# LSH attention, MoE and a dense SoLU layer on one core: all dense layers behind the last MoE

## Chip, core and metric

The kernel runs on one core of one Trainium2 chip. The metric is the device time of one execution in microseconds (us). The engines of the core are TensorE (PE, with its weight loads listed apart as PEld), VectorE (DVE), ScalarE (ACT), GpSimd (POOL) and SyncE (SP), which issues the DMAs. In the profile all of the kernel's instructions carry one line, L391 (the helper that emits them; L396 in the changed kernel), so groups of instructions are told apart by the names of their tiles.

## The reference

Three layers follow one another. Attention takes 2 x 8 heads of 768 rows with head width 64; a pair of row and column counts only where both fall in the same bucket of six sign bits. Its output, 1536 rows of 512, goes through four experts, and then through the dense layer.

```python
mask = q_bucket[:, :, :, None] == k_bucket[:, :, None, :]     # sign bits of q @ proj, k @ proj
scores = np.where(mask, scale * (q @ k.T), -1e9)
x = softmax(scores) @ v                                       # -> [1536, 512]

p = domain_probs / (domain_probs.sum(-1, keepdims=True) + 1e-09)
for e in range(4):                                            # w1 512 x 1024, w2 1024 x 512
    y += p[:, e:e + 1] * (np.maximum(x @ w1[e], 0) @ w2[e])

h = y @ w_in                                                  # 512 x 1024
solu = h * softmax(h)
ln = (solu - mean(solu)) / np.sqrt(var(solu) + 1e-06) * g_ln
out = ln @ w_out                                              # 1024 x 512
```

w_in, w_out and g_ln come as 64-bit floats, which the kernel decodes with integer operations into 32-bit ones; all else is float32.

## The kernel before

**Chunks.** The 1536 rows are worked on in four chunks of three tiles of 128 rows (`CHUNKS`, line 20), called 0 to 3 here. For each chunk there are three stages: attention (`attn_steps`, 1082), MoE (`moe_a`, 1277, the first product and the relu; `moe_b`, 1328, the second product and the sum over experts), and the dense layer. The main loop (1597 to 1660) runs MoE(c), then dense(c), and so on. The attention of a later chunk is laid between their steps by `Fill` (1561): attention(1) runs beside MoE(0), attention(2) beside dense(0) and MoE(1), attention(3) beside dense(1) and MoE(2). Attention(0) comes first, with nothing beside it but the loads.

**Pairs.** A product of float32 matrices is made of three matmuls of float16 halves: high times high, high times low, low times high. A matrix is split by a scaled copy to float16 (ACT, POOL or DVE) and a subtraction of the copy from the original (DVE). Scales come from row or matrix maxima (`amax`, 603; `fit_to`, 606, turns a column of maxima on PE into one factor). In chunk 0 the MoE runs with unsplit scales: its weights are kept as 32-bit pairs, and the largest of each expert is taken in passing (`wm`), so that the later chunks can use float16.

**Attention.** A row tile of one head is a row of 768 scores in PSUM. DVE takes the maximum (`sm<-PS`), ACT the exponential into `p`, then come a scaled copy `hl` in float16, a fused DVE instruction for the low half (`hl<-p,sm,hl`, scaling and subtraction in one), and a DMA that turns both halves into `t`. There are two `hl` buffers (`hl16_r`, 486) and three of `t`. When three rows stand turned, 12 short products with the values give the head's output, `xp`. So 24 rows make a chunk.

**Weights.** Two streams (`Stream`, 1181) load raw weights in pieces of 512 KB (`wra`, `wrb`), two buffers each, and split each into halves (`wsa`, `wsb`; as float16 `wsa0h`, `wsa1h` and so on, four slots each, `ws16_r`, 518). Every chunk loads and splits the MoE's 32 pieces, and the dense layer's eight: four of `winD`, four of `woutD`.

**Dense layer of chunks 0 to 2.** `y_fit` (1352) scales the rows of y by their maxima; `y_transposes` (1363) turns them on PE (`idn,y`, four 128x128 turns a tile) and splits them out of PSUM. `h2_piece` (1389) makes the first product; `ln_tiles` (1408) makes the exponential (`ee`), the softmax and the LayerNorm (`ln`) for the three tiles at once. For chunks 0 and 1 `ln_a` (1473) turns ln on PE (`idn,ln`), `ln_b` (1485) makes the second product; for chunk 2 `ln_turn` (1449) turns ln by DMA instead. While `ln_tiles` runs, the first steps of MoE(c+1) and of attention give PE work. Chunk 3 has a function of its own, `last_layer` (1501), which works tile by tile.

**Decoding.** `decode_a` and `decode_b` (1167, 1177) decode w_in and w_out beside MoE(0) and dense(0), and write them to memory as `winD` and `woutD`, from where each chunk loads them.

**Order.** The operations are recorded in program order and sent out by `emit` (376) in an order that a table of numbers sets (`ORDER`). Further tables choose the engine where an operation has several forms ("AVG": ACT, DVE or POOL) and the PSUM bank. Each engine works through its own instructions in that order; a waiting instruction holds up all that follow on its engine.

Of the kernel before, what the change touches and what calls it, by code (L numbers as in the profile page):

```python
# [8 lines left out]
F32 = mybir.dt.float32  # L9
# [386 lines left out]
def lsh_attention_moe_solu(  # L396
# [30 lines left out]
    TURN = 2  # L427
# [1267 lines left out]
```

## Time and profile before

| | before |
|---|---|
| median of 3 runs | 902.07 us (900.07 to 903.45) |
| profiled execution, whole | 897.96 us |
| its span | 895.8 us |
| PE busy | 852.7 us (95%) |
| DVE busy | 752.4 us (84%) |
| ACT busy | 488.2 us (54%) |
| mean granted clock of TensorE | 0.983 |

The profile is one execution. A busy time counts the time in which an engine had an instruction running; matmuls overlap, so their mean durations add up to more than the time between their starts. "Idle before" is the time in which an engine stood still ahead of an instruction, and the name behind "<-" is what released it. DMA share is the mean busy share of the core's 16 DMA engines. The granted clock is a share of TensorE's full speed.

In time, the stages of before are: attention(0) to about 120 us, MoE(0) with attention(1) to about 330, dense(0) from there, the others after it, and the last dense layer from about 860.

### The profile page before, as it was taken

The numbers are of one execution on the slowest core, as the hardware profiler recorded it, in microseconds if no ns is written. First come the engines' busy times: TensorE is split into PE (matmuls) and PEld (weight loads), VectorE is DVE, ScalarE is ACT, GpSimd is POOL, SyncE is SP. The second block draws the span as 40 slices with busy tenths as digits, with TensorE's granted clock in tenths as the row PEclk, the third lists the DMA queues.
The fourth block names the chain that finished last, engine by engine and source line by source line (L and its number), as shares of the span: only waits on it lengthen the run. The fifth ranks groups of instructions, "written<-read, shape, count | busy, mean of one in ns | idle before, by whom it ended". The sixth has DMA issues, their size and how long they took to land.

```text
span 895.8 us, 13401 instructions
## 1 busy us (share of the span) xinstructions
PE 852.7 (95%) x4549; PEld 547.0 (61%) x4549; DVE 752.4 (84%) x1377; ACT 488.2 (54%) x894; POOL 250.6 (28%) x302
## 2 busy tenths in 40 slices
PE   6889899998899996999999999999999999999998
PEld 5778699876688553555566555555565555455543
DVE  6888898998999999878899889887887687556595
ACT  4798346567775676644485558544463365212232
POOL 2556443554545111333224202102230010101110
PEclk9699999999999997999999999999999999999999
DMA  7877778999999887769999979587968347733400
GB/s 179 243 187 193 268 236 198 265 259 260 233 276 327 280 270 243 191 178 265 248 227 250 277 199 239 150 227 222 236 150 188 116 141 175 220 134 118 165 24 36
DMA packets 224916, 185.67 MB, mean 207 GB/s; under 512 B 137424, under 2 KB 190032, under 8 KB 224848
## 3 DMA queue, kind: packets, MB, share of 16 engines
q1 hardware_dynamic: 224848, 184.82, 75.7%
q8 instruction: 36, 0.59, 0.3%
q14 instruction: 32, 0.26, 0.1%
HBM read 128.68 MB, written 19.73 MB: 166 GB/s over the span
## 4 chain that ended last, share of the span: by engine, by line
PE 72%; DVE 12%; ACT 5%; issue 4%; DMA 3%; POOL 2%; SPq 2%; POOLq 0%; DVEq 0%; ACTq 0%
PE PS L391 72%; DVE ln L391 2%; DVE sm L391 2%; SPq L391 2%; ACT p L391 1%; DVE st L391 1%; POOL sm L391 1%; DMA t<-in_v_dram 1%; DVE hl L391 1%; DMA wrb<-in_moe_w_dram 1%; DMA t320h<-hl 1%; DMA t<-hl 1%; DVE wm L391 1%; DVE y L391 1%; ACT ee L391 1%
## 5 line engine op out<-in xcount | busy, mean ns | idle before, releaser
L391 ACT ACTIVATE p<-PS,sm 128x768 f32<-128x768 f32 x96 | 95.0, 990 | 32.8 <-DVE sm L391 22.5
L391 DVE TENSOR_REDUCE sm<-PS 128x1 f32<-128x768 f32 x96 | 91.0, 950 | 18.2 <-PE PS L391 17.5
L391 POOL TENSOR_SCALAR sm<-sm 128x1 f32<-128x1 f32 x113 | 51.7, 457 | 179.5 <-DVE sm L391 139.9
L391 PEld LDWEIGHTS <-wsa1h 128*128 128x128 f16 x576 | 55.7, 98 | 40.4 <-issue 1.2
L391 PEld LDWEIGHTS <-wsa0h 128*128 128x128 f16 x576 | 55.5, 98 | 39.4 <-issue 1.3
L391 DVE SCALAR_TENSOR_TENSOR hl<-p,sm,hl 128x768 f16<-128x768 f32 x72 | 72.7, 1011 | 5.8 <-ACT hl L391 3.8
L391 ACT ACTIVATE hha0h<-PS 128x384 f16<-128x384 f32 (+1 forms) x79 | 38.1, 492 | 72.1 <-PE PS L391 72.1
L391 PEld LDWEIGHTS <-hha0h 128*128 128x128 f16 x484 | 44.7, 98 | 50.0 <-issue 4.6
L391 PE MATMUL PS<-wsb1h,hha0h 128*128 128x512 f16 x248 | 73.9, 380 | 0.0
L391 PE MATMUL PS<-kB,qB 80*128 80x384 f32 x192 | 67.2, 350 | 6.2 <-DMA qB<-qD 3.7
L391 PE MATMUL PS<-xh,wsa 128*128 128x384 f32 x256 | 70.2, 340 | 1.9 <-POOL wsa L391 0.9
L391 PE MATMUL PS<-wsb0h,hha0h 128*128 128x512 f16 x236 | 70.4, 380 | 0.9 <-ACT y L391 0.8
L391 PE MATMUL PS<-xh1h,wsa1h 128*128 128x384 f16 x256 | 67.5, 326 | 0.0
L391 PE MATMUL PS<-xh1h,wsa0h 128*128 128x384 f16 x256 | 67.2, 326 | 0.0
L391 PE MATMUL PS<-kC,qC 128*128 128x384 f32 x144 | 57.2, 397 | 6.0 <-ACT p L391 5.5
L391 DVE SCALAR_TENSOR_TENSOR hxa0h<-PS,hha0h 128x384 f16<-128x384 f32 x64 | 35.0, 551 | 24.2 <-ACT hha0h L391 23.8
L391 ACT ACTIVATE sm<-sm 128x1 f32<-128x1 f32 x96 | 23.4, 249 | 47.8 <-POOL sm L391 24.2
L391 PEld LDWEIGHTS PS<-xh,wsa 128*128 128x128 f32 x256 | 46.6, 188 | 4.4 <-POOL wsa L391 1.6
L391 DVE SCALAR_TENSOR_TENSOR wsb0h<-wrb,fit,wsb0h 128x1024 f16<-128x1024 f32 x32 | 41.8, 1306 | 7.8 <-ACT wsb0h L391 7.4
L391 DVE SCALAR_TENSOR_TENSOR wsa1h<-wra,fit,wsa1h 128x1024 f16<-128x1024 f32 x32 | 41.0, 1282 | 7.4 <-POOL wsa1h L391 4.1
L391 PE MATMUL PS<-wsb1h,hxa0h 128*128 128x512 f16 x124 | 47.0, 379 | 0.0
L391 DVE SCALAR_TENSOR_TENSOR wsb1h<-wrb,fit,wsb1h 128x1024 f16<-128x1024 f32 x32 | 40.9, 1278 | 6.9 <-POOL wsb1h L391 4.7
(301 smaller groups left out, 2241.2 us busy)
## 6 DMA issues: line engine op xcount, KB each, us to landing
wra<-in_moe_w_dram SPq DMA_DIRECT2D x64, 512.0 KB, 5.0
wrb<-in_moe_w_dram SPq DMA_DIRECT2D x64, 512.0 KB, 4.4
kC<-kD SPq DMA_DIRECT2D x24, 384.0 KB, 4.7
wra<-winD SPq DMA_DIRECT2D x16, 512.0 KB, 5.3
wrb<-woutD SPq DMA_DIRECT2D x16, 512.0 KB, 4.6
vr<-in_v_dram SPq DMA_DIRECT2D x30, 192.0 KB, 4.5
kB<-kD SPq DMA_DIRECT2D x24, 240.0 KB, 4.4
qD<-stk SPq DMA_DIRECT2D x27, 192.0 KB, 3.1
```

The costliest lines, as they stand in the source:

```text
L391: fn(**{key: self.now(x) for key, x in kw.items()})
```

## The change

All four dense layers stand behind MoE(3) in one function, `dense`. It runs over the 12 tiles one after the other: `first(i)` makes the first product, the softmax and the LayerNorm of a tile, `second(i)` its output product, two tiles later (`lag = 2`). Four pieces of `winD` and four of `woutD` are loaded and split once, and stay in the eight `ws16_r` slots. `y_fit` now writes the scaled rows of y as a pair of float16 halves, as soon as a tile's MoE is done, and two DMAs turn them; ln is copied and subtracted into halves and turned by two DMAs in each tile but the last, whose ln PE turns. `y_transposes`, `h2_piece`, `ln_turn`, `ln_a`, `ln_b` and `last_layer` are gone.

Decoding is one pass of 16 units beside MoE(3), through the `ln` buffer. The scales of the MoE and dense weights come from sums of squares (ACT or DVE) with one small matmul in `fit_norm`, in place of maxima with a turn. In attention, `p` is scaled in place, copied to float16, and subtracted, as three instructions (scaling and copy on ACT, DVE or POOL, subtraction on DVE or POOL), in place of a scaled copy and a fused subtraction. `Fill` spreads the attention of a chunk over the steps of one MoE alone, attention(2) over MoE(1) and attention(3) over MoE(2), since no dense layer stands between them. MoE(3) has no attention beside it, as before.

The instructions on PE that turn y go from 57 to 9, those that turn ln from 90 to 26. DVE's instructions go from 1297 to 1378, counted as the order below counts them.

**The order on DVE, at the last rows of attention(2).** `p` holds exponentials, `hl` a row's float16 halves, `sm` row sums and maxima, `vr` raw values, `hxa` the relu's low half, `wra`/`wrb` raw weights, `ys` the row maxima of y. Before:

```order
L391 TENSOR_SCALAR hl_81<-p_78,sm_90 128x768
L391 TENSOR_REDUCE sm_92<-PS 128x1
L391 RECIPROCAL sm_91<-sm_91 128x1
L391 SCALAR_TENSOR_TENSOR hl_81<-p_78,sm_90,hl_81 128x768
L391 SCALAR_TENSOR_TENSOR hxa0h<-PS,hha0h 128x384
L391 SCALAR_TENSOR_TENSOR wsb1h<-wrb_103,fit,wsb1h 128x1024
L391 TENSOR_SCALAR hl_80<-p_79,sm_91 128x768
L391 SCALAR_TENSOR_TENSOR hl_80<-p_79,sm_91,hl_80 128x768
L391 SCALAR_TENSOR_TENSOR wsa1h<-wra_101,fit,wsa1h 128x1024
L391 RECIPROCAL sm_92<-sm_92 128x1
L391 SCALAR_TENSOR_TENSOR xp_98<-PS,tmp_99 64x384
L391 TENSOR_TENSOR hl_65<-vr_73,hl_65 128x3x64
```

And after:

```order
L396 CAST hl_80<-p_78 128x768
L396 TENSOR_TENSOR hl_80<-p_78,hl_80 128x768
L396 RECIPROCAL sm_91<-sm_91 128x1
L396 TENSOR_TENSOR hl_65<-vr_73,hl_65 128x3x64
L396 CAST hl_81<-p_79 128x768
L396 RECIPROCAL sm_92<-sm_92 128x1
L396 TENSOR_TENSOR hl_81<-p_79,hl_81 128x768
L396 CAST hl_80<-p_77 128x768
L396 TENSOR_TENSOR hl_80<-p_77,hl_80 128x768
L396 SCALAR_TENSOR_TENSOR xp_97<-PS,tmp_99 64x384
L396 CAST hl_65<-vr_73 128x3x64
L396 TENSOR_REDUCE ys<-y_112 128x1
```

Before, splits of MoE weights and the relu's halves stand between the rows; after, the last rows stand in a row, behind the last instruction of MoE(1), and the maximum of a y tile follows them.

**The order on PE, from the first product of the dense layer to its output product.** `xh1h` and `xl1h` are the halves of the turned y, `wsa1h` of w_in, `wsb0h` of w_out; `hha0h` and `t_82` hold turned ln. Before, in the last layer, where the turns of ln follow the products of the third tile:

```order
L391 LDWEIGHTS xh1h
L391 MATMUL PS<-wsa1h,xh1h 128x512
L391 LDWEIGHTS xl1h
L391 MATMUL PS<-wsa1h,xl1h 128x512
L391 MATMUL PS<-idn,ln_113 128x128 x4
L391 LDWEIGHTS hha0h
L391 MATMUL PS<-wsb0h,hha0h 128x512
```

And after, at the first output product:

```order
L396 LDWEIGHTS xh1h
L396 MATMUL PS<-wsa1h,xh1h 128x512
L396 LDWEIGHTS xl1h
L396 MATMUL PS<-wsa1h,xl1h 128x512
L396 LDWEIGHTS t_82
L396 MATMUL PS<-wsb0h,t_82 128x512
```

The turns on PE are gone from between the two products; ahead of the rows after stand 144 matmuls of the first product, six tiles, before the output product of the first.

The diff, cut to its core (`ORDER` and the other two tables are new throughout):

```diff
--- before.py
+++ after.py
 ORDER = """
-3 14 0 12 13 12 1 43 43 21 0 37 20 1 11 22 20 16 20 4 16 10 16 29 26 15 15 1 8 1 13 22 4 19 11 10 58 10 16 5
...
+3 0 12 12 0 11 22 0 21 25 10 11 23 5 18 13 1 33 17 16 17 10 1 14 15 26 14 21 7 13 1 6 1 19 1 9 4 16 8 12 4 2 2
...
-    XA, WA = 16.0, 4.0
+    XA, WA, YA = 16.0, 160.0, 16.0
...
+    def squares(out, in_):
+
+        n = in_.shape[1]
+        d = dump_r.next()[:, 0:n]
+        forms = dict(
+            A=("activation", dict(out=d, in_=in_, func=ACTF.Square, accum_out=out)),
+            V=(
+                "scalar_tensor_tensor",
+                dict(out=d, in0=in_, scalar=1.0, in1=in_, op0=ALU.mult, op1=ALU.mult, accum_out=out),
+            ),
+        )
+        rec.add([(name, *forms[name]) for name in "AV"])
...
+    def fit_norm(x, j, limit):
+
+        n, m = x.shape[1:]
+        ps = a_b.next()[:, 0:n * m]
+        b, t = big[:, j:j + n], fit[:, j:j + n]
+        T.matmul(out=ps, lhsT=one, rhs=x, start=True, stop=True)
...
-        yT[c] = tuple(t.bitcast(F16)[:, :, 0:TM] for t in x)
+        lower, upper = (tuple(flat16(t)[:, i * KD * TM:(i + 1) * KD * TM].rearrange("p (k q) -> p k q", k=KD) for t in x) for i in range(2))
+        yT[c] = upper if c < 2 else lower
         if c:
-            xT[c] = yT[c]
+            xT[c] = lower
...
                 hl16 = hl16_r.next()
                 h16, l16 = hl16[:, 0], hl16[:, 1]
-                times_by("AGV", h16, p, st[:, 4:5])
-                V.scalar_tensor_tensor(out=l16, in0=p, scalar=st[:, 4:5], in1=h16, op0=ALU.mult, op1=ALU.subtract)
+                times_by("AGV", p, p, st[:, 4:5])
+                copy_by("AGV", h16, p)
+                sub_by("VG", l16, p, h16)
                 o = rr * 128
                 SP.dma_start_transpose(
                     out=d16.rearrange("p a r q -> p (a r) q")[:, :, o:o + 128],
...
-            amax(dm[:, cols[i]:cols[i] + 1], w)
+            squares(dm[:, cols[i]:cols[i] + 1], w)
...
-        return decode_steps(units + out_units(0, OUT0, n), n, ln_r.next().rearrange("p a n -> p (a n)"), range(12))
-
-    def decode_b():
-        return decode_steps(out_units(OUT0, NF2, 256), 256, y_r.next().rearrange("p a n -> p (a n)"), range(12, 20))
+        return decode_steps(units + out_units(0, NF2, n), n, ln_r.t[0].rearrange("p a n -> p (a n)"), range(16))
...
-                    amax(wm[:, 2 * e + self.kind - 1, i:i + 1], t, AX.XY)
+                    squares(wm[:, 2 * e + self.kind - 1, i:i + 1], t.rearrange("p a n -> p (a n)"))
...
+        add_moe1(c, 0, NP)
+        add_moe2(c, 0, NP)
+    for j in range(FF2 // 256):
+        i1["in", j] = len(W1.items)
+        W1.items.append(winD[j])
+    for j in range(NF2 // 2):
+        i2["out", j] = len(W2.items)
+        W2.items.append(woutD[j])
...
     def y_fit(c, t):
         y = y_t[c][:, t]
-        top, by, back = (ys[:, c % 2, i, t:t + 1] for i in range(3))
+        top, by = (ys[:, c, i, t:t + 1] for i in range(2))
         amax(top, y)
-        V.tensor_scalar(out=top, in0=top, scalar1=1e-30, scalar2=1.0 / XA, op0=ALU.max, op1=ALU.mult)
+        V.tensor_scalar(out=top, in0=top, scalar1=1e-30, scalar2=None, op0=ALU.max)
         V.reciprocal(out=by, in_=top)
-        times_by("AVG", y, y, by)
-        if c == NC - 1:
-            V.tensor_tensor(out=by, in0=by, in1=fit[:, NM:NM + 1], op=ALU.mult)
-        V.tensor_tensor(out=back, in0=top, in1=big[:, NM:NM + 1], op=ALU.mult)
-
-    def y_transposes(c, t, ps):
+        power(by, by, YA)
+        V.reciprocal(out=top, in_=by)
+        y16 = hl16_r.next()[:, :, 0:DM]
+        times_by("AVG", y16[:, 0], y, by)
+        less_by("V", y16[:, 1], y, by, y16[:, 0])
+        for a in range(2):
+            SP.dma_start_transpose(out=yT[c][a][:, :, t * 128:t * 128 + 128], in_=y16[:, a])
...
-    def y_transposes(c, t, ps):
...
-    def h2_piece(c, j):
...
-    def ln_turn(c):
...
-    def ln_a(c, s):
...
-    def ln_b(c, s):
...
-    def last_layer(c):
...
+    def dense():
+
+        o_b = Bank(PS, 1, range(8), 2)
         t_b, h2_b = Bank(PS, 1, range(8), 3), Bank(PS, 2, (6, 4, 0, 2), 3)
+        tiles = [(c, t) for c in range(NC) for t in range(chunks[c][2])]
+        ln, mx = ln_r.t[0], mx_r.t[0]
+        for j in range(FF2 // 256):
+            W1.split(i1["in", j])
         parts = {}
 
+        def first(i):
+            c, t = tiles[i]
+            if t == 0:
+                V.tensor_scalar(out=ys[:, c, 1], in0=ys[:, c, 1], scalar1=fit[:, NM:NM + 1], scalar2=None, op0=ALU.mult)
+                V.tensor_scalar(out=ys[:, c, 2], in0=ys[:, c, 0], scalar1=big[:, NM:NM + 1], scalar2=None, op0=ALU.mult)
             h = h2_b.next()
+            m = mx[:, i % NT]
             for j in range(FF2 // 256):
                 h2_mm(c, t, j, h[:, j // 2])
                 if j % 2 == 1:
+                    V.tensor_reduce(out=m[:, j // 2:j // 2 + 1], in_=h[:, j // 2], axis=AX.X, op=ALU.max)
             hv = h.rearrange("p a n -> p (a n)")
+            l = ln[:, i % NT]
+            ln_tiles(m.unsqueeze(1), [(hv, l, l, hv)], [ys[:, c, a, t:t + 1] for a in (1, 2)])
+            if i < len(tiles) - 1:
+                x = t16_r.t[i % 3].rearrange("p a r q -> p (a r q)")
+                x16, y16 = x[:, 0:2 * FF2], x[:, 2 * FF2:4 * FF2].rearrange("p (a k q) -> p a k q", a=2, q=128)
+                hi, lo = x16[:, 0:FF2], x16[:, FF2:2 * FF2]
+                copy_by("AVG", hi, l)
+                sub_by("VG", lo, l, hi)
+                for a, y in enumerate((hi, lo)):
+                    SP.dma_start_transpose(out=y16[:, a], in_=y)
+                parts[i] = [[y16[:, a, k] for a in range(2)] for k in range(NF2)]
+            else:
+                gh, gl = (cuts(x[0], 512) + cuts(x[1], 512) for x in (hh_t, hx_t))
+                parts[i] = []
+                for g in range(2):
+                    ps = t_b.next()
+                    with rec.group():
+                        for a in range(4):
+                            k = g * 4 + a
+                            T.transpose(out=ps[:, a * 128:a * 128 + 128], in_=l[:, k * 128:k * 128 + 128], identity=idn)
+                    acopy(gh[g], ps)
+                    sub(V, gl[g], ps, gh[g])
+                    parts[i] += [[y[g][:, a * 128:a * 128 + 128] for y in (gh, gl)] for a in range(4)]
+
+        def second(i):
+            c, t = tiles[i]
             o = o_b.next()
+            for k in range(NF2):
+                wh, wl = W2.get(i2["out", k // 2])
+                hh, hl = parts[i][k]
+                with rec.group():
+                    for m, (a, w) in enumerate(((hh, wh), (hh, wl), (hl, wh))):
+                        T.matmul(out=o, lhsT=a, rhs=w[:, k % 2, :], start=(k == 0 and m == 0), stop=(k == NF2 - 1 and m == 2))
             store(c, t, o)
+
+        lag = 2
+        for i in range(len(tiles) + lag):
+            if i < len(tiles):
+                first(i)
+            if i >= lag:
+                second(i - lag)
...
+        if c == NC - 1:
+            dec_it = decode()
+        for s in range(NS):
+                fill.start(c + 2, NS - 1)
+            if c == NC - 1 and s % DI == 0:
+                next(dec_it, 0)
+            if c == NC - 1 and s == 17:
+                fit_norm(dm[:, 0:8].unsqueeze(1), NM, WA)
+    for _ in dec_it:
+        pass
+    fit_norm(dm[:, 8:16].unsqueeze(1), NM + 1, WA)
+    V.tensor_scalar(out=ob, in0=big[:, NM + 1:NM + 2], scalar1=1.0 / P10, scalar2=None, op0=ALU.mult)
+    dense()
```

## Rows read from the trace of the kernel before

**Rows 1.** The page's busy times: time, share of the span, instructions.

```profile
PE 852.7 (95%) x4549; PEld 547.0 (61%) x4549; DVE 752.4 (84%) x1377; ACT 488.2 (54%) x894; POOL 250.6 (28%) x302
```

**Rows 2.** Stretches: length; PE, PEld, DVE, ACT, POOL busy us (instructions); clock; DMA share; GB/s.

```profile
0.00:120.00 120.00, 100.60 (x536) 85.62 (x537) 101.83 (x196) 74.62 (x158) 59.48 (x96) 0.91 0.80 219
...
160.00:260.00 100.00, 90.08 (x461) 73.85 (x460) 94.54 (x167) 70.66 (x137) 53.57 (x46) 1.00 1.02 254
...
340.00:360.00 20.00, 11.99 (x52) 7.31 (x50) 18.71 (x59) 12.43 (x27) 3.36 (x4) 0.74 0.75 235
360.00:540.00 180.00, 179.85 (x986) 103.34 (x987) 155.40 (x261) 100.68 (x183) 53.18 (x73) 1.00 0.90 231
540.00:700.00 160.00, 158.78 (x864) 89.82 (x863) 137.53 (x235) 83.53 (x152) 27.18 (x33) 1.00 0.80 204
700.00:860.00 160.00, 160.00 (x844) 82.70 (x843) 106.47 (x160) 56.40 (x84) 14.87 (x13) 1.00 0.46 143
860.00:896.00 36.00, 31.42 (x156) 15.31 (x154) 25.16 (x86) 12.21 (x20) 0.84 (x2) 1.00 0.06 23
```

**Rows 3.** Groups on PE: tiles, shapes, count, busy us, mean ns, idle before.

```profile
L391 PE MATMUL PS<-idn,ln 128*128 128x128 f32 x90 | 15.4, 307 | 5.4 <-DVE ln L391 4.2 <-DVE wsa L391 1.0
...
L391 PE MATMUL PS<-idn,y 128*128 128x128 f32 x57 | 8.6, 274 | 0.0
```

**Rows 4.** Timeline of PE at a turn of y: start us, length us, instruction.

```profile
302.52 0.38 PE L391 MATMUL PS<-wsa1h,xl0h 128*128 128x512 f16 x1
302.74 0.60 PE L391 MATMUL PS<-idn,y 128*128 128x128 f32 x4
303.17 0.59 PE L391 MATMUL PS<-wsa1h,xh0h 128*128 128x512 f16 x2
```

**Rows 5.** Chain of waits, 176 to 260 us: start us, length us, what ran.

```profile
177.65 5.90 DMA t320h<-hl
...
239.11 5.84 DMA t<-hl
```

**Rows 6.** Groups on DVE and ACT over the span, columns as in rows 3.

```profile
L391 DVE SCALAR_TENSOR_TENSOR wsa1h<-wra,fit,wsa1h 128x1024 f16<-128x1024 f32 x32 | 41.0, 1282 | 7.4 <-POOL wsa1h L391 4.1 <-ACT wsa1h L391 3.2
L391 DVE TENSOR_REDUCE wm<-wrb 128x1 f32<-128x1024 f32 x16 | 19.4, 1209 | 0.2 <-DMA wrb<-in_moe_w_dram 0.2
L391 DVE TENSOR_REDUCE wm<-wra 128x1 f32<-128x1024 f32 x16 | 19.3, 1208 | 2.4 <-DMA wra<-in_moe_w_dram 2.4
L391 DVE SCALAR_TENSOR_TENSOR ln<-ln 128x512 int32<-128x512 int32 (+1 forms) x24 | 17.6, 738 | 1.0 <-ACT ln L391 0.9
L391 DVE SCALAR_TENSOR_TENSOR hl<-p,sm,hl 128x768 f16<-128x768 f32 x72 | 72.7, 1011 | 5.8 <-ACT hl L391 3.8 <-POOL hl L391 1.6
L391 DVE TENSOR_SCALAR hl<-p,sm 128x768 f16<-128x768 f32 x21 | 12.9, 614 | 1.8 <-DMA t<-hl 1.6
L391 DVE TENSOR_TENSOR ln<-ln,ee 128x1024 f16<-128x1024 f32 x3 | 3.7, 1223 | 0.1
L391 ACT ACTIVATE p<-PS,sm 128x768 f32<-128x768 f32 x96 | 95.0, 990 | 32.8 <-DVE sm L391 22.5 <-POOL sm L391 7.4 <-DVE hxa0h L391 0.7
```

**Rows 7.** Maxima of score rows on DVE, in 140 to 240 and 360 to 500 us.

```profile
L391 DVE TENSOR_REDUCE sm<-PS 128x1 f32<-128x768 f32 x19 | 17.9, 948 | 2.4 <-PE PS L391 2.4
...
L391 DVE TENSOR_REDUCE sm<-PS 128x1 f32<-128x768 f32 x23 | 21.8, 951 | 7.3 <-PE PS L391 7.2
```

**Rows 8.** Turns of `hl`, all of the span: from issue to landing.

```profile
DMA to landing us min/median/max: 3.6/4.8/8.2
```

**Rows 9.** Chain of waits, 334 to 361 us, columns as in rows 5.

```profile
340.30 1.24 ACT ee L391 x2
...
351.82 0.82 DVE ln L391
```

**Rows 10.** Chain of waits, 860 us to the end.

```profile
873.76 0.60 DVE mx L391
...
884.56 7.58 PE PS L391 x38
```

More of the change, by code (lines that the diff above doesn't have):

```diff
@@ L559, in sub_by, with ops_by @@
         rec.add([(name, "tensor_tensor", dict(out=out, in0=a, in1=b, op=ALU.subtract)) for name in names])
+    def ops_by(names, out, in_, a, b, op0, op1):
+        args = dict(out=out, in0=in_, scalar1=a, scalar2=b, op0=op0)
+        if op1 is not None:
+            args.update(op1=op1)
+        rec.add([(name, "tensor_scalar", args) for name in names])
     def less_by(names, out, in_, by, b):
@@ L604, in amax @@
         V.tensor_reduce(out=out, in_=in_, axis=axis, op=ALU.max, apply_absolute_value=True)
[L606 to L621 removed]
+    dump_r = Ring(0, tiles=[flat16(t32_r.t[0])[:, 2 * R * TM + i * 1024:2 * R * TM + i * 1024 + 1024] for i in range(4)])
@@ new lines, in fit_v @@
+    def fit_v(b):
+        ts = [t.rearrange("p a r q -> p (a r q)").bitcast(F32)[:, 0:H // 2 * R * D] for t in t16_r.t[0:2]]
+        for i, t in enumerate(ts):
+            SP.dma_start(
+                out=t.rearrange("p (h x) -> p h x", h=H // 2),
+                in_=v[b, i * H // 2:(i + 1) * H // 2].rearrange("h (p r) d -> p h (r d)", r=R),
+            )
+            amax(vm[:, i:i + 1], t)
+        ps = a_b.next()
+        j = 2 * E + b
+        x, y, top = big[:, j:j + 1], fit[:, j:j + 1], vm[0:1, 2:3]
+        V.tensor_reduce(out=x, in_=vm[:, 0:2], axis=AX.X, op=ALU.max)
+        T.transpose(out=ps[0:1, 0:128], in_=x, identity=idn)
+        V.tensor_reduce(out=top, in_=ps[0:1, 0:128], axis=AX.X, op=ALU.max)
+        V.tensor_scalar(out=top, in0=top, scalar1=1e-30, scalar2=None, op0=ALU.max)
+        T.matmul(out=ps[:, 256:257], lhsT=one[0:1], rhs=top, start=True, stop=True)
+        V.reciprocal(out=y, in_=ps[:, 256:257])
+        power(y, y, XA)
+        V.reciprocal(out=x, in_=y)
+        if b:
+            for e in range(E):
+                fit_p(b, e)
@@ L636, in fit_w @@
     def fit_w(e):
[L637 removed]
+        fit_norm(wm[:, 2 * e:2 * e + 2], 2 * e, WA)
         fit_p(0, e)
[L640 to L652 removed]
     def consts_a():
@@ L1210, in split @@
                 if c:
-                    w = [x.rearrange("p (a n) -> p a n", a=t.shape[1]) for x in ws16_r[self.kind].next()]
+                    w = ws16_r[self.kind].next()
+                    w = [x.rearrange("p (a n) -> p a n", a=t.shape[1]) for x in w]
                     j = NM + self.kind - 1 if m is None else m // (NF // 2) * 2 + self.kind - 1
@@ L1385, in h2_mm, with ln_tiles @@
                     m += 1
[L1387 to L1408 removed]
+    def ln_tiles(mx, tiles, back):
         n = len(tiles)
@@ L1471, in store @@
         SP.dma_start(out=out[b * S:(b + 1) * S].rearrange("(p r) d -> p r d", r=R)[:, r0 + t], in_=ot)
-    def ln_a(c, s):
-        n = chunks[c][2]
-        if c == TURN:
-            g, i = divmod(s, NF2 // 2)
-            hT["l", c, s] = [turned[g][:, a, i, 0:128 * n] for a in range(2)]
-            return
-        ps = h_b.next()
-        with rec.group():
-            for t in range(n):
-                T.transpose(out=ps[:, t * 128:(t + 1) * 128], in_=ln_t[c][:, t, s * 128:(s + 1) * 128], identity=idn)
-        hT["l", c, s] = split_h(ps, 128 * n, False)
@@ L1485, in ln_b @@
-    def ln_b(c, s):
-        b, r0, n = chunks[c]
-        m, j = divmod(s, 2)
-        i = i2["out", c, m]
-        w = W2.get(i)
-        hh, hl = hT.pop(("l", c, s))
-        mm2(("l", c), range(n), hh, hl, w, j, s == 0, s == NF2 - 1)
-        if s == NF2 - 1:
-            for t in range(n):
-                o = acc["l", c][t]
-                store(c, t, o)
-        if j == 0:
-            W2.split(i + 1)
-        else:
-            W2.load(i + 2)
-    def last_layer(c):
-        n = chunks[c][2]
-        ln_t[c] = ln_r.next()
-        mx_t[c] = mx_r.next()
-        y_b, o_b = Bank(PS, 1, range(8), 1), Bank(PS, 1, range(8), 2)
+    def dense():
+        o_b = Bank(PS, 1, range(8), 2)
@@ L1507, in last_layer @@
         t_b, h2_b = Bank(PS, 1, range(8), 3), Bank(PS, 2, (6, 4, 0, 2), 3)
-        gh, gl = (Ring(0, tiles=cuts(x[0], 512) + cuts(x[1], 512)) for x in (hh_t, hx_t))
+        tiles = [(c, t) for c in range(NC) for t in range(chunks[c][2])]
+        ln, mx = ln_r.t[0], mx_r.t[0]
+        for j in range(FF2 // 256):
+            W1.split(i1["in", j])
         parts = {}
-        def transposes(t):
-            parts[t] = []
-            for g in range(2):
-                ps = t_b.next()
-                with rec.group():
-                    for i in range(4):
-                        s = g * 4 + i
-                        T.transpose(
-                            out=ps[:, i * 128:i * 128 + 128], in_=ln_t[c][:, t, s * 128:(s + 1) * 128], identity=idn
-                        )
-                hh, hl = gh.next()[:, 0:512], gl.next()[:, 0:512]
-                acopy(hh, ps)
-                sub(V, hl, ps, hh)
-                parts[t].append((hh, hl))
@@ L1538, in last_layer @@
-        for t in range(n):
-            if t == 0:
-                transposes(0)
-            if t + 1 < n:
-                transposes(t + 1)
-            o = o_b.next()
-            for g in range(2):
-                hh, hl = parts[t][g]
-                for i in range(4):
-                    s = g * 4 + i
-                    wh, wl = W2.get(i2["out", c, s // 2])
-                    with rec.group():
-                        for m, (a, w) in enumerate(((hh, wh), (hh, wl), (hl, wh))):
-                            T.matmul(
-                                out=o,
-                                lhsT=a[:, i * 128:i * 128 + 128],
-                                rhs=w[:, s % 2, :],
-                                start=(s == 0 and m == 0),
-                                stop=(s == NF2 - 1 and m == 2),
-                            )
-            store(c, t, o)
+            l = ln[:, i % NT]
@@ L1597, in lsh_attention_moe_solu @@
     fill.start(1, NS - 10)
-    a0 = 0
     for c in range(NC):
-        end = NS - (LB if c == NC - 1 else 0)
-        for s in range(a0, end):
+        if c == NC - 1:
+            dec_it = decode()
+        for s in range(NS):
             if s == NS - LA and c + 1 < NC:
-                fill.start(c + 2, NS + 1)
+                fill.start(c + 2, NS - 1)
             a_to(c, s + LA + 1)
```

222 lines of the change are left out of this document (45 added, 177 removed), and 205 rows, old and new, of the table ORDER.

## Prediction

> **What bounds the kernel now.** I read the page's busy shares first. TensorE (PE) is busy 852.7 of 895.8 us and VectorE (DVE) 752.4 [rows 1], so two things can shorten the kernel: less PE work, or fewer stalls of PE. The table by stretches says where the stalls are [rows 2]: PE idles 19 us in the first 120 us (the first chunk's attention, which the change leaves alone), 9.9 us in 160 to 260, 8.0 us in 340 to 360, and 4.6 us in the last 36. From 360 to 860 it is idle 1.4 us in 500, so there every microsecond saved must come out of PE's own instructions, and any new stall is paid in full.
>
> The two stalls differ. In 160 to 260 DVE is busy 94.5 of 100 us and the DMA share stands at its ceiling, 1.02; the chain of waits goes through 5.9 us landings of attention rows [rows 5]. In 340 to 360 the chain runs through the LayerNorm of chunk 0, from an exponential at 340.30 to the last scaling at 351.82 [rows 9], while the work meant to cover it has run out; the granted clock falls to 0.74 there.
>
> The sum is made against the profiled execution: span 895.8 us, 897.96 us with what lies around it. The median of the three runs, 902.07, is 4.1 above that; I add it at the end.
>
> **The change part by part.**
>
> *Turns taken from PE.* Gone are 48 transposes of y and 64 of ln (90 to 26 and 57 to 9 in the order). Four in a row take from 302.74 to 303.17, so 0.108 us each [rows 4], and 112 are 12.1 us. The busy column would give 0.15 and 0.17 each [rows 3], 18 us in all, but that counts waits and overlap. They stand in stretches where PE does not idle, so all of it counts: **-12** (-18 to -12). The matrix work of the dense layers is the same.
>
> *Weights split once.* 24 loads of 512 KB and 24 splits go, some 31 us of DVE (1.28 each [rows 6]) plus the scaling on ACT or POOL. After 360 PE is the bound, so there this gives nothing by itself.
>
> *Chunk 0's stage relieved.* Out of the first MoE go 38.7 us of maxima over weights (now mostly squares on ACT) and the decoding, whose largest DVE group is 17.6 us [rows 6]. Against that stand ten more subtractions of weight halves at some 1.2 us each. From the first to the last score row of chunk 1 the order holds 134 us of DVE work before and 107 after (counts times the mean durations of the trace; small instructions overlap, so the busy time is some 8% less), while PE has 604 matmuls before and 670 after, 121 us at the spacing of an unstalled stretch (986 in 180 us [rows 2], 0.18 each). DVE stops being the bound. The stall of 9.9 us, with some 4 us of refilling after its many stops, goes for the most part: **-11** (-14 to 0). What is late next is PE itself.
>
> *Chunk 0's LayerNorm stall.* Nothing dense stands in the middle any more, so the 8.0 us of idling and 2 to 3 us at the fallen clock go: **-11** (-12 to -8).
>
> *Attention packed tighter.* This is the new cost. Before, the rows of chunk 2 ran beside dense(0) and MoE(1), 23 of them from 360 to 500 [rows 7], 6.1 us each. After, PE's order between the first and last score of chunk 2 holds only 433 matmuls instead of 709, 78 us of work or 3.3 us a row, and the last six rows stand behind the last matmul of MoE(1) (the order section shows DVE there: casts and subtractions in a row with nothing of MoE between). DVE's work for the same 24 rows, counted the same way, is 91 us. Of that, the new subtraction in place of the fused one (1.01) is bounded by that row and by 0.75 of 1.22, the same subtraction at 1024 columns [rows 6]; I take 0.97, and 0.61 for the cast from the scaling of equal shape. One row also holds one of two hl slots for cast 0.6, subtraction 1.0 and a landing of 4.8 [rows 8], so the ring allows 3.2 us a row, 77 us. So 88 to 91 us for 78: 10 to 13 us of stall. Behind it waits the whole of MoE(2): its first 72 matmuls need all eight heads. The drain after the last score (maximum 0.95 [rows 7], exponential 0.99 [rows 6], scaling, cast and subtraction 2.5, landing 4.8, 12 products 2, evacuations and small steps 3: some 14 us, with 7 us of PE work behind it) lies in the same stretch. **+12** (0 to +40). The rows of chunk 3 have 694 matmuls, 125 us of PE, for 113 of DVE: **+3** (0 to +8) for the drain at the end of MoE(2).
>
> *Decoding moved to the last MoE.* In 700 to 860 DVE was busy 106.5 of 160 and the DMA share 0.46 [rows 2]. The order gives DVE 112 us there for 130 us of PE: hidden. If that cover failed, up to 50 us of DVE work would show.
>
> *The dense tail.* Twelve tiles of 48 matmuls at 0.22 us [rows 4], 10.4 us a tile on PE. DVE needed 25 us for the three tiles of the last layer [rows 2], 8.4 each, so PE remains the bound. A tile's chain takes some 11 us (from the second maximum at 873.76 to the first transposes at 884.56 [rows 10]); with copy, subtraction and landing it is 18 to 19 us, against 20 us of other tiles between its two halves. PE starts with six tiles of first products, before any output product (order, second place), while the output weights are split; that start may leave **+4** (0 to +12). The SP queue gets 34 more DMA turns and 24 fewer loads; in the tail it has little else. The end is as before: the last tile still turns on PE, with 14 us of output products in front.
>
> The Trainium skill speaks against this part: the page "VectorE: DVE Perf Modes", section "The three transpose paths", gives a 128x128 turn as 390 ns on TensorE and 1309 ns by DMA, and its rules prefer TensorE where PSUM will do as destination. At 1309 ns one after another, the 272 blocks now turned by DMA for y and ln would be an estimate of 356 us. The trace disagrees: 12 blocks land in 4.8 us, 0.40 each.
>
> **Sum.** 895.8 - 12 - 11 - 11 + 12 + 3 + 4 = 881 us of span, 883 with the 2.2 around it, **887** at the level of the median, 1.7% less than before. What a measurement of this kernel can tell from no change is about 0.5%, 4.5 us.
>
> **The rivals.**
>
> *Landings bound the packed rows (slower).* If the row transposes of chunk 2 land not in 4.8 but in 8.2 us, the longest seen [rows 8], a row takes (1.6 + 8.2) / 2 = 4.9 us, 24 rows 118 us instead of 90. That is +28: 909 us of span, 915 at the median. It starts to cost above 5.9 us and makes the kernel slower by over 0.5% above some 7.4. For it: where rows ran fastest before, 19 in 100 us, the DMA share was 1.02 and landings of 5.9 us stood on the chain [rows 2, 5, 7]; no stretch of this trace shows rows at 3.7 us. Against: decoding and dense weights no longer load in that stage. Chance 0.14.
>
> *The stalls stay.* Chunk 0's stage keeps its 11 us because the DMA share, not DVE, holds it, and the row stall is some 16: 881 + 11 + 4 = 896 of span, 902 at the median, no change. For it: 1.02 in 160 to 260. Against: DVE's 94.5 there. Chance 0.14.
>
> *No new stall (faster still).* The rows keep up because PE's work slips behind them without idling, and dense starts smoothly: 881 - 16 = 865, 871 at the median. For it: 360 to 540 ran with DVE at 86% and a DMA share of 0.90 without a stall [rows 2]. Against: 91 us of DVE in 78. Chance 0.15.
>
> *The DMA turns pace the tail.* Two turns a tile at 8.2 us each, one behind the other, are 16.4 against 10.4: six us for eleven tiles, 66, so 953. The DMA share of 0.46 and 0.06 at the end [rows 2] speaks against it. Chance 0.03.
>
> The forecast has 0.54. The range takes in the row stall from nothing almost to the slow rival's price: 869 to 912. Faster by over 0.5% (below 897.6): nearly all of the forecast and the fast rival, 0.70. Within 0.5%: 0.15. Slower: 0.15.
>
> **What would show it.** Right: no y transposes on PE past the first chunk; PE idle in the first MoE behind 120 us near 2 us; no clock dip at a LayerNorm in the middle; one stall of about 10 us at the end of the second MoE, with PE waiting for kC, kB or t; the tail at 10.4 us a tile and near 100% PE. Wrong: hl landings above 7 us there, a row pace above 4.5 us, or PE idle between dense tiles released by turned t tiles or by wsb. The forecast fails most easily in the size of that one stall, since nothing in this trace ran so tight.

## The result, and the profile after

The changed kernel takes 879.99 us (median of 4 runs, 879.61 to 880.84) against 901.07 us for the kernel before (median of 4, 899.82 to 903.45): a ratio of 0.976, 95% interval 0.974 to 0.979. It is 2.4% faster; 887 us had been forecast, with a range of 869 to 912. The profiled execution took 880.03 us with a span of 878.2, against 897.96 and 895.8 before; so the span is 17.6 us shorter. Its busy times, from the page:

```profile
PE 835.6 (95%) x4431; PEld 534.6 (61%) x4431; DVE 723.5 (82%) x1468; ACT 492.2 (56%) x896; POOL 301.7 (34%) x331
```

Beside [rows 1]: PE's busy time fell by 17.1 us, its idle time only from 43.1 to 42.6. That looks as if the stalls had not mattered. The table by stretches (length; PE, PEld, DVE, ACT, POOL busy; granted clock; DMA share; GB/s) shows that they moved:

```profile
0.00:120.00 120.00, 98.78 (x545) 84.44 (x546) 93.85 (x190) 79.47 (x168) 55.38 (x89) 0.97 0.77 211
...
160.00:260.00 100.00, 99.45 (x520) 87.72 (x519) 83.85 (x150) 74.05 (x137) 51.43 (x47) 1.00 0.94 238
260.00:340.00 80.00, 79.05 (x469) 46.92 (x468) 68.31 (x120) 34.87 (x61) 19.93 (x22) 1.00 0.89 255
340.00:400.00 60.00, 58.35 (x312) 33.76 (x311) 50.88 (x95) 38.04 (x66) 20.68 (x26) 0.97 0.91 243
400.00:450.00 50.00, 44.17 (x222) 27.01 (x220) 46.50 (x89) 38.52 (x73) 19.13 (x28) 0.90 1.00 222
450.00:500.00 50.00, 42.15 (x227) 23.66 (x228) 38.77 (x76) 18.63 (x35) 14.23 (x16) 0.90 0.85 231
500.00:600.00 100.00, 100.00 (x550) 58.60 (x549) 82.50 (x142) 64.40 (x115) 44.58 (x47) 1.00 0.98 237
...
760.00:800.00 40.00, 40.00 (x187) 18.18 (x186) 37.86 (x136) 17.81 (x28) 2.60 (x3) 1.00 0.35 76
800.00:878.00 78.00, 73.67 (x345) 33.60 (x343) 48.91 (x175) 24.13 (x37) 14.86 (x8) 1.00 0.47 100
```

In 160 to 260, where PE stood 9.9 us before [rows 2], it now stands 0.55 us and does 59 more matmuls, with DVE at 84 instead of 94.5. The dip of the clock at 340 to 360 is gone. In its place there is one new stall, at the end of attention(2); 500 to 800 has no idle time at all, and the last 78 us have 4.3 us of it, about as much as the end had before (4.6 us [rows 2]). The new stall lies almost wholly in 30 us:

```profile
400.00:430.00 30.00, 29.85 (x162) 17.86 (x160) 27.88 (x50) 23.66 (x44) 11.62 (x16) 1.00 1.00 247
430.00:460.00 30.00, 17.13 (x74) 10.86 (x73) 25.59 (x54) 18.76 (x37) 9.53 (x17) 0.69 0.98 187
```

PE stands 12.9 of 30 us there, at a clock of 0.69. What it waits for between 395 and 500 us (the four longest sums; total, times, longest):

```profile
PE PS L396 <- DVE xp L396: 5.4, 1, 5.4
PE PS L396 <- ACT p L396: 3.9, 6, 1.3
PE PS L396 <- DVE hl L396: 1.8, 1, 1.8
PE PS L396 <- ACT stk L396: 1.5, 2, 0.8
```

The wait for `xp` belongs to the drain, the time from the last rows to their first use: the product of the next to last head goes into the PSUM bank that the head before it used (bank 2 in the table), and the instruction that empties it stands on DVE behind the last three rows. These rows wait for an `hl` slot, that is for the landing of the row two before, as DVE's timeline shows in brackets (idle before, and what ended it). PE's timeline follows, from MoE(1)'s last matmul over the last scores (`kC,qC`) and the products of the last two heads to MoE(2)'s first matmul:

```profile
450.62 0.56 DVE L396 CAST hl<-p 128x768 f16<-128x768 f32 x1 [0.57 <-DMA t320h<-hl]
...
453.47 0.56 DVE L396 CAST hl<-p 128x768 f16<-128x768 f32 x1 [0.97 <-DMA t320h<-hl]
...
456.35 0.56 DVE L396 CAST hl<-p 128x768 f16<-128x768 f32 x1 [1.33 <-DMA t<-hl]
```

```profile
428.41 0.38 PE L396 MATMUL PS<-wsb1h,hxb0h 128*128 128x512 f16 x1
...
440.50 0.69 PE L396 MATMUL PS<-kC,qC 128*128 128x384 f32 x1 [0.60 <-ACT p L396]
...
458.55 3.59 PE L396 MATMUL PS<-t320h,vs2h 128*128 128x384 f16 x12 [5.37 <-DVE xp L396]
...
462.61 2.12 PE L396 MATMUL PS<-t,vs0h 128*128 128x384 f16 x12
...
464.75 0.34 PE L396 MATMUL PS<-xh0h,wsa0h 128*128 128x384 f16 x1
```

The casts come 2.85 and 2.88 us apart; two slots held for 0.6 + 1.0 us and a landing of 4.1 would give (1.6 + 4.1) / 2 = 2.85. MoE(2) begins at 464.75. The wait for `xp` hides another behind it: the turn of the very last row was issued at 457.93 and landed 3.7 us later, at 461.6, so the last head's product could not have begun more than 1.0 us before its 462.61. The landings themselves were no longer than before (rows of 355 to 460 us, from issue to landing):

```profile
DMA to landing us min/median/max: 3.7/4.1/6.5
```

### The profile page after: what moved, and what is told of

Read it like the earlier page. It is cut to its first block, busy times and chain, and to the rows that moved or that the text cites. A ratio compares the mean times of both kernels' runs of the same rounds, so it can differ in the third digit from the quotient of the medians.

```text
span 878.2 us, 13299 instructions
## 1 busy us (share of the span) xinstructions
PE 835.6 (95%) x4431; PEld 534.6 (61%) x4431; DVE 723.5 (82%) x1468; ACT 492.2 (56%) x896; POOL 301.7 (34%) x331
## 5 line engine op out<-in xcount | busy, mean ns | idle before, releaser
L396 POOL TENSOR_SCALAR sm<-sm 128x1 f32<-128x1 f32 x104 | 44.7, 430 | 127.8 <-DVE sm L396 90.2
L396 PEld LDWEIGHTS <-hha0h 128*128 128x128 f16 x400 | 37.1, 98 | 40.7 <-issue 3.7
L396 PE MATMUL PS<-wsb1h,hha0h 128*128 128x512 f16 x200 | 60.0, 382 | 0.0
L396 PE MATMUL PS<-wsb0h,hha0h 128*128 128x512 f16 x200 | 59.6, 380 | 0.0
L396 POOL TENSOR_SCALAR ln<-ln 128x512 int32<-128x512 int32 x23 | 29.0, 1262 | 78.3 <-DVE ln L396 66.8
L396 DVE TENSOR_TENSOR hl<-p,hl 128x768 f16<-128x768 f32 x50 | 50.4, 1008 | 5.8 <-ACT hl L396 3.7
L396 POOL TENSOR_TENSOR hl<-p,hl 128x768 f16<-128x768 f32 x22 | 38.3, 1746 | 23.4 <-ACT hl L396 11.4
L396 POOL TENSOR_SCALAR p<-p,sm 128x768 f32<-128x768 f32 x33 | 32.6, 990 | 35.9 <-DVE sm L396 31.4
L396 PE MATMUL PS<-xl,wsa 128*128 128x384 f32 x128 | 43.5, 340 | 0.1
L396 PE MATMUL PS<-xl1h,wsa1h 128*128 128x384 f16 x128 | 42.2, 330 | 0.0
```

The source lines that it names most:

```text
L396: fn(**{key: self.now(x) for key, x in kw.items()})
```

## The experiments

All times are medians; the changed kernel's 879.99 is called 880.0. The ratio of each to the kernel before comes from runs on the same chip. "Order" means the order in which instructions are sent to the engines, which a table sets: where an edit is one of the order, the same instructions are sent, and PSUM banks are given out anew where they must be.

**The price of a turn on PE.** Eight turns of a constant ahead of each output product:

```diff
                 with rec.group():
+                    for a in range(8 if k == 0 else 0):
+                        T.transpose(out=o[:, a % 4 * 128:a % 4 * 128 + 128], in_=idn, identity=idn)
                     for m, (a, w) in enumerate(((hh, wh), (hh, wl), (hl, wh))):
```

> The changed kernel with eight more 128x128 turns of a constant on PE in each of the twelve output products of the dense tail, 96 in all; their result is overwritten by the product. PE has no idle time there. By the spacing of 0.108 us: +10.4, 890.4 us. By the mean busy durations of the groups (0.15 to 0.17): +14.4 to +16.3, 894 to 896. If turns were hidden beside other work: 880.

Measured 887.56 us (886.63 to 889.31; ratio 0.985, 0.982 to 0.988): +7.6, so 0.08 us a turn. In the profiled executions, from 640 us to the end, PE's busy time grew by 9.96 us, 0.104 a turn:

```profile
640.00:888.00 248.00, 243.63 (x1261) 124.72 (x1258) 193.54 (x505) 97.91 (x161) 52.38 (x37) 1.00 0.52 146
```

For the changed kernel, 640 to 878, the same row has 233.67. The spacing [rows 4], 0.108, is the right price or a little too high; the busy time of a group by its count [rows 3], 0.15 to 0.17, is too high. The 112 turns that went are worth 9 to 12 us.

**Three hl slots.**

```diff
+    hl16_r.t.append(ee_r.t[0].bitcast(F16)[:, 0:2 * S].rearrange("p (a n) -> p a n", a=2))
```

> The changed kernel with three hl slots instead of two (the third lies in the buffer of the exponential, which the changed kernel no longer needs behind attention(0)). Theory of the ring (a row holds one of two slots for copy, subtraction and landing, (0.6 + 1.0 + 4.0) / 2 = 2.8 us a row, and the last copies of attention(2) came 2.9 us apart behind landings): the last three rows draw together by about 1 us each and the small stalls before them shrink, 875 to 877. Rival (the order of the instructions on DVE and ACT sets the drain): 879 to 881.

Measured 875.79 (875.00 to 876.74; ratio 0.972, 0.969 to 0.975): the ring is a part of the new stall, 4.2 us of it, as expected. In the profiled executions the gain lies in that stage: from the first exponential of attention(2) to the first of attention(3) it is 126.7 us (356.5 to 483.2) instead of 131.4 (355.7 to 487.1), and in 430 to 460 PE is busy 19.75 us instead of 17.13. A fourth slot for `p` as well:

```diff
+    p4_r = Ring(0, tiles=p_r.t + [ln_r.t[0][:, 0, 0:S]])
...
-                p, st = row(U, rr, s_b, V)
+                p, st = row(U, rr, s_b, V, p4_r if c < 3 else p_r)
```

> The changed kernel with three hl slots and four p slots in attention(1) and (2) (the fourth lies in the LayerNorm's buffer, which is free until the decoding). Three hl slots alone gave 875.8. PE waited 3.9 us in six places for ACT's exponential between 395 and 500 us, and ACT for a p slot that a subtraction still read. Theory (slots hold the packed rows): 872 to 875. Rival (three hl slots took what there was): 875 to 877.

Measured 874.69 (872.51 to 877.09; ratio 0.972, 0.968 to 0.976): 1.1 us less than three slots alone, with ranges that overlap, so nothing is shown for `p`.

**DVE's work in the packed rows.**

```diff
-                sub_by("VG", l16, p, h16)
+                w = slice(0, S // 8 if c == 2 else S)
+                sub_by("VG", l16[:, w], p[:, w], h16[:, w])
```

> The changed kernel, but the subtraction that makes the low half of a score row works on an eighth of the columns in attention(2); the rest of the low half is left as an earlier row left it. It takes about 0.8 us of DVE (or 1.5 us of POOL) from each of 24 rows, some 16 us of DVE over the stage, and leaves order, DMAs and buffers as they are. Theory (the packed rows of attention(2) are paced by DVE, 88 to 91 us of its work beside 78 us of PE work): most of the PE idling between 380 and 480 us goes, 864 to 870 against 880. Rival (they are paced by the chain of one row through two hl slots and its landing, where a shorter subtraction saves 0.8 of 5.6 us in two slots, 0.4 us a row over the rows that the ring holds): 874 to 877.

Measured 875.11 (873.59 to 877.06; ratio 0.972, 0.967 to 0.976). DVE's busy time in 400 to 450 fell from 46.5 to 39.3 us, but PE's idle time in 400 to 500 only from 13.7 to 12.4 us:

```profile
400.00:450.00 50.00, 42.50 (x218) 25.96 (x215) 39.26 (x90) 39.98 (x77) 14.09 (x28) 0.92 1.03 218
450.00:500.00 50.00, 45.11 (x240) 25.86 (x241) 37.93 (x76) 18.17 (x32) 14.95 (x15) 0.91 0.89 242
```

The gain of 4.9 us lies in the range of the chain through the slots (874 to 877), and not in that of DVE's work (864 to 870); it is about what the third slot gave. So the amount of DVE's work does not pace the packed rows. That the gain comes from the shorter chain is argued, since the edit takes work from DVE and shortens the chain at once.

**The row as before the change** (scaled copy and fused subtraction, 72 instructions fewer):

```diff
-                times_by("AGV", p, p, st[:, 4:5])
-                copy_by("AGV", h16, p)
-                sub_by("VG", l16, p, h16)
+                times_by("AGV", h16, p, st[:, 4:5])
+                V.scalar_tensor_tensor(out=l16, in0=p, scalar=st[:, 4:5], in1=h16, op0=ALU.mult, op1=ALU.subtract)
```

> The changed kernel with the row of attention(1) to (3) as before the change: one scaled copy to float16 and one fused scaling and subtraction on DVE, in place of scaling in place, copy, and subtraction. 72 scalings go (33 from ACT, 21 from POOL, 18 from DVE), 22 subtractions move from POOL to DVE: DVE gets some 12 us more, the chain of a row one instruction less, about 0.9 us. If DVE's work paces the packed rows: 883 to 890 against 880. If the chain of a row does (a slot of p is held for one instruction less): 875 to 879.

Measured 886.50 (886.11 to 889.19; ratio 0.985, 0.981 to 0.989), +6.5. It can't be read as the price of the row, though it lies in the range for DVE's work. In the profiled execution (889.19, so 9.2 above the changed kernel's) 5.6 us lie ahead of the first row of attention(1) (137.1 instead of 131.5 us), in attention(0), whose code is the same; 2.9 us of them are a wait of PE for a DMA, and why is not known. In the packed stage, from the first exponential of attention(2) to the first of attention(3), both kernels take 131.4 us.

**Attention(2) earlier in the order**: every instruction of attention(2) 12 us of PE work earlier, or only its first rows.

> The changed kernel with every instruction of attention(2) standing about 12 us of PE work earlier in the order against MoE(0) and MoE(1); nothing else is changed. Theory (the new stall is the end of attention(2), which stands behind the last matmul of MoE(1) with nothing to cover its drain): the last rows and the turn of the last head now have some 12 us of MoE(1) matmuls beside them, so most of the 13.7 us of PE idling between 400 and 500 us and of the fallen clock behind it goes: 862 to 870 us against 880. Rival (the rows cannot run earlier, since DVE is the limit from 260 us on): the stall moves or stays, 877 to 883.

> The changed kernel with the rows of attention(2) beginning 12 us of PE work earlier but ending at the same place of the order, so 24 rows over 90 us of PE work instead of 78. If the stall is the pace (DVE needs 88 to 91 us for rows that have 78 us of PE work beside them, the working of the prediction): 866 to 870. If it is the drain of the last rows, which is where it was: only the small stalls before 430 us go (3.6 and some 3 us), 874 to 878.

Measured 938.82 (936.28 to 941.04; ratio 1.043, 1.038 to 1.047) and 918.04 (917.08 to 919.11; ratio 1.019, 1.016 to 1.022). Both miss both expectations. The exponentials of attention(2) (shortest, median, longest ns; first and last start) in the first of the two:

```profile
L396 ACT ACTIVATE p<-PS,sm x24: 984/990/991, 359.3 to 486.0; 128x768 f32<-128x768 f32 x24
```

In the changed kernel they run from 355.7 to 450.6. Put earlier in the order, the rows did not come earlier in time, and PE was busy only 50.2 us between 340 and 400, where it had been 58.35. It waited 2.9 us for the evacuations of the projection (160 to 340), 2.9 for a load that comes after it (340 to 500), and 16.7 for exponentials (340 to 500). The explanation that the rows were put ahead of what they need, and then held up what stood behind them, fits these waits but is not tested. The two runs say nothing on pace or drain; they show that this order can't be shifted without being planned again.

**The projection of attention(3) out of the last rows.** In the changed kernel the exponentials of the last two rows stand on ACT behind evacuations of that projection (`stk`), which wait for PE:

```profile
448.92 0.87 ACT L396 ACTIVATE stk<-PS 128x384 fp32r<-128x384 f32 x2 [1.87 <-PE PS L396]
449.68 1.00 ACT L396 ACTIVATE p<-PS,sm 128x768 f32<-128x768 f32 x1
...
450.65 1.00 ACT L396 ACTIVATE p<-PS,sm 128x768 f32<-128x768 f32 x1
```

The edit on ACT (PE, DVE and POOL likewise):

```diff
 L396 ACTIVATE sm_90<-sm_90 128x1
-L396 ACTIVATE stk_67<-PS 128x384
 L396 ACTIVATE p_78<-p_78,sm_90 128x768
-L396 ACTIVATE hl_65<-vr_73 128x3x64
-L396 ACTIVATE stk_67<-PS 128x384
-L396 ACTIVATE stk_66<-PS 128x384
 L396 ACTIVATE p_79,sm_91<-PS,sm_91 128x768
 L396 ACTIVATE p_77,sm_92<-PS,sm_92 128x768
+L396 ACTIVATE p_77<-p_77,sm_92 128x768
+L396 ACTIVATE tmp_99<-PS 64x384
 L396 ACTIVATE hl_65<-vr_73 128x3x64
-L396 ACTIVATE p_77<-p_77,sm_92 128x768
-L396 ACTIVATE tmp_99<-PS 64x384
+L396 ACTIVATE stk_67<-PS 128x384
...
```

> The changed kernel with one place of its order altered: 24 instructions of the projection of attention(3) on PE, ACT, DVE and POOL, which stood among the last rows of attention(2), stand directly behind the instructions of these rows; 73 places of the order differ. In the trace of the changed kernel the exponentials of the last two rows, whose scores were done at 442, begin at 449.7 and 450.6, behind two evacuations of that projection on ACT, which wait for turns on PE that stand behind the product of head 5, and so for a landing. Theory (this knot in the order is the larger part of the drain): the last rows come 4 to 7 us earlier, 872 to 876 against 880. Rival (the drain is set by the hl slots and the landings, the exponentials only wait in front of that): 878 to 881.

> Three hl slots (875.8 alone) together with the altered place of the order. If slots and knot hold different parts of the drain, the gains add up: 866 to 872. If both took away the same wait: 873 to 876.

Measured 885.00 (884.20 to 885.97; ratio 0.983, 0.979 to 0.986) and 883.93 (882.68 to 885.02; ratio 0.982, 0.979 to 0.985). The last exponential of the first did come 2.7 us earlier (447.9), but PE then stood 10.5 us in one piece (8.3 with three slots) for halves that the projection needs, ahead of the products of the last two heads. Once more, now behind these products:

> Three hl slots, and the projection of attention(3) moved once more: now it begins behind the products of the last two heads on PE, and runs out between the first products of MoE(2) (130 places of the order differ). In the run before that moved it directly behind the rows (883.9 with three slots), PE stood 8 to 10 us for the projection's halves on DVE, ahead of the last two heads' products. Theory (the last rows' exponentials were held up by the projection's evacuations, and the loss of the run before was only the new wait in front of the two products): 868 to 873 against 875.8. Rival (the projection fills the gap of the drain, so wherever it goes it costs its chain of some 2 us a head, now ahead of MoE(2)): 878 to 886.

Measured 885.26 (883.72 to 888.66; ratio 0.984, 0.982 to 0.986). PE now stood 8.7 us for `xp`, where it had been 3.1 with three slots, and then for the projection among MoE(2)'s first products:

```profile
450.68 4.00 PE L396 MATMUL PS<-t320h,vs2h 128*128 128x384 f16 x12 [8.67 <-DVE xp L396]
...
468.68 0.69 PE L396 MATMUL PS<-stk,lhs_w 128*128 128x384 f32 x1 [3.79 <-DVE ys L396]
```

Of three placings of the projection the first is the best; that it fills the drain there, and elsewhere costs its own chain, fits both runs. How much an order planned as a whole could take out of the remaining stall stays open. One thing was seen only afterwards and not tried: with bank 0, which is free by then, for the next to last head, its product would not wait for `xp` (5.4 us here, 3.1 with three hl slots). But the last head's product would still wait for its last row: the estimate from the landings is a gain of at most 1.0 us here (461.6 against 462.61), and 2.7 with three slots (456.8 against 459.5).

**Decoding back beside the first MoE**, in two orders:

```diff
-            squares(dm[:, cols[i]:cols[i] + 1], w)
+            squares(dm[:, cols[i]:cols[i] + 1], w, dec_r)
```

(`dec_r` is a dead buffer of its own; the rest of the edit is the order.)

> The changed kernel with the 176 instructions of the decoding moved back beside the first MoE (about 120 to 330 us, spread evenly), all else in its order; the sums of squares of the decoding write their dead output to another buffer. It undoes the relief of that stage: some 48 us of DVE work (41 instructions of 0.42, 32 of 0.68, 13 of 0.7 us) and 24 DMAs come into 210 us where DVE had about 35 us to spare. Theory (the stall of 9.9 us was DVE's, and the relief took it away): the stall comes back, 890 to 900 against 880. Rival (it was the maxima alone, or nothing of this, and decoding hides there as well as anywhere): 879 to 883. In the last MoE, which loses the 48 us, nothing should be gained if the decoding was hidden there.

> The changed kernel with the decoding back beside the first MoE, spread more finely than in the run before that gave 931.8: each of the 16 units over 9.5 us of PE work, from about 140 to 300 us, so that it does not fall into the beginning of attention(2). 48 us of DVE work come to a stretch in which DVE had some 27 us to spare. Theory (that stage is bound by DVE when the decoding is in it): PE idles again between 160 and 300 us and the time is 890 to 905 against 880. Rival (the 52 us of the run before came only from the beginning of attention(2), and the stage itself has room): 879 to 885.

Measured 931.77 (930.73 to 932.58; ratio 1.035, 1.031 to 1.039) and 937.81 (937.31 to 941.01; ratio 1.042, 1.039 to 1.046): +52 and +58, far over what was expected. The two put the decoding in different places, as one of its groups on DVE shows (first and last start at the end), the first run's and then the second's:

```profile
L400 DVE TENSOR_SCALAR ln<-ln x41: 407/420/1861, 220.7 to 400.4; 128x512 int32<-128x512 int32 x41
```

```profile
L400 DVE TENSOR_SCALAR ln<-ln x41: 408/419/1141, 129.0 to 344.9; 128x512 int32<-128x512 int32 x41
```

The first was meant to spread it evenly from 120 to 330 us, but most of it came behind the last row of attention(1) (264.5 us). It hardly touches the place of the old stall: attention(1)'s rows took 133.0 us from the start of the first exponential to that of the last (131.5 to 264.5), where the changed kernel takes 129.1 (131.5 to 260.6), and the loss came between them and the first row of attention(2), 146.0 us (to 410.5) instead of 95.1 (to 355.7). In the second, attention(1)'s rows took 181.3 us (129.2 to 310.5); the stall is back in its old place, and much larger:

```profile
160.00:260.00 100.00, 81.08 (x370) 68.57 (x370) 81.59 (x139) 60.21 (x119) 54.38 (x44) 0.90 0.83 220
260.00:340.00 80.00, 65.75 (x315) 50.71 (x316) 71.30 (x123) 49.37 (x94) 35.80 (x35) 0.87 0.89 241
```

```profile
DVE ln L400 <- POOL ln L400: 9.8, 5, 4.0
```

DVE is busy only 81.6 of 100 us: it is not full, it waits in its order (9.8 us for POOL's part of the decoding between 160 and 300), and all that stands behind waits with it. So the stage does not take the decoding in this order, but the kernel before carried it there with a stall of 9.9 us, in an order made for it; how the relief divides between decoding and maxima is not shown. Nor is it shown whether DVE or the DMAs held the old stall, since the change takes load from both (in 160 to 260 DVE went from 94.5 to 83.9 us, the DMA share from 1.02 to 0.94). At the other end the answer is clear. From the last exponential of attention(3) to the end of the span it is 269.2 us with the decoding in the last MoE (609.0 to 878.2), and without it 269.4 (661.0 to 930.4) and 269.4 (666.6 to 936.0): there it is hidden whole.

## Why the prediction was right, and where its terms were not

**Where the stalls were** held: DVE-laden rows of attention(1) and the LayerNorm of chunk 0, both read from [rows 2] and [rows 9], are gone. The first was put at -11; 59 more matmuls in the same 100 us, at the 0.18 us of the prediction, are 10.6. That DVE was what held it stays argued: the rival in the prediction, the DMA share, fell with it. The second, -11, is 8.0 us of idling and 3 at the low clock (an estimate: 12.0 busy us at 0.74 [rows 2]).

**Turns**, -12: shown by the added turns to be 9 to 12. From 120 us on, PE has eight turns of ln and none of y:

```profile
L396 PE MATMUL PS<-idn,ln 128*128 128x128 f32 x8 | 1.0, 272 | 0.0
```

**The new stall** stood where it had been said, at the end of attention(2) with MoE(2) behind it, but the term was mis-sized and its reason wrong. Where 12 us had been put, PE was idle 15.3 us between 340 and 500 (1.65 + 5.83 + 7.85); with an estimate of 5.3 us for the clock of 0.69 on 17 busy us in 430 to 460, and some 2 for the smaller dips beside it (0.83 in 380 to 390, 0.92 in 460 to 470), it is up to 23. The step that failed is "91 us of DVE in 78": with 14.3 us of DVE's work taken away (723.5 to 709.2 us over the span), PE's idle time in 400 to 500 went only from 13.7 to 12.4 us. The rows took 94.9 us from first to last exponential, close to the 88 to 91 forecast, but while MoE(1) gave PE work they kept up. The stretch from the first exponential to MoE(1)'s last matmul, with 17 of the 24 rows, has 1.8 us of idle time, and the one from there to MoE(2) has 12.9 (columns as in the table by stretches):

```profile
355.70:428.80 73.10, 71.30 (x379) 41.55 (x378) 64.42 (x117) 54.12 (x97) 29.23 (x36) 0.98 0.96 239
428.80:464.75 35.95, 23.08 (x104) 14.63 (x105) 29.17 (x61) 20.19 (x41) 10.65 (x18) 0.72 0.97 198
```

So what stops PE is the drain behind MoE(1)'s last matmul. It was counted at 14 us from the last score, with 7 of PE work behind it; from the start of the last scores (440.5) to MoE(2) (464.75) it is 24, of which PE idles 9.3. The ring's formula, (1.6 + landing) / 2, was a bound of pace in the prediction; in the drain it holds to 0.03 us, and a third slot is worth 4.2 us.

**Attention(3), dense start**, +3 and +4: PE idled 0 us in 500 to 640, and 0.7 us from there to 862, which takes in MoE(3) and the dense layers up to their last 16 us. Some 6 us were too many.

**Landings as a rival** fell: median 4.1, longest 6.5, where 8.2 had been its case. The turns in the dense tail landed in 3.2 us at the median, and PE hardly idled there, so they paced nothing. The Trainium skill's rule to turn on TensorE where PSUM will do (page "VectorE: DVE Perf Modes", section "Rules for kernel authors") did not pay here: eight blocks in 3.2 us are 0.40 us each beside matmuls, where the page's table (section "The three transpose paths") has 1309 ns for one, and PE, which the rule prefers, is the engine that had no time to spare.

**The sum.** 881 us of span were forecast, 878.2 came. By the measured terms, with 12 for the turns, it is 895.8 - 12 - 10.6 - 11 + 15.3 to 23 + 0.7, less 1.4 for the idle time of 360 to 860 that is gone: 877 to 884 (up to 3 more with 9 for the turns). That the sum fits is in part luck: a stall put too low by 3 to 11 against two terms put too high by 6. Of the 7 us between 887 and 880, 4.1 are none of these: they were added because the runs before lay that far above their profiled execution, and the new ones do not (879.99 against 880.03).

## What to carry to other kernels

When a filler between two stages is taken out, cost the drain of what stood in it (last row to first use, with every buffer slot and landing on the way) before the throughput of its engines; here the throughput gave the rows' length rightly and the stall's place wrongly. Price an instruction that goes by the distance between starts in an unstalled stretch, not by the busy time of its group. And do not read a shifted order as an undo: the same instructions, 12 us of PE work earlier, cost 59 us.

## What had not been expected of the hardware

The turns of rows landed sooner in the packed stage (4.1 us at the median, against 4.8 for the rows of attention(2) before, and 4.8 over the whole span [rows 8]), though the DMA share there was 0.91 to 1.00; why is not shown. The granted clock fell to 0.60 in 440 to 450 and 0.57 in 450 to 460 (2.4 GHz is full speed, and the lower level, 1.2 GHz, half of that), after PE had waited 0.3 to 0.7 us ahead of every few instructions from 431 on, and the twelve matmuls of a head's product then took 3.9 us instead of 2.1:

```profile
432.79 2.11 PE L396 MATMUL PS<-t,vs0h 128*128 128x384 f16 x12 [0.68 <-ACT stk L396]
...
444.29 3.92 PE L396 MATMUL PS<-t,vs1h 128*128 128x384 f16 x12
```
